# Column product of the Fourier layers: seven block products for two row tiles instead of eight

## The chip, the cores and the metric

The kernel runs on one core of one Trainium2 chip. The time is the device time of one launch in microseconds, the median of several runs. TensorE (PE) multiplies, VectorE (DVE), ScalarE (ACT) and GpSimd (POOL) do the elementwise work, and SyncE's queue (SP) starts all transfers.

## The reference

Four layers on x (2048 rows, 640 columns): attention, Fourier, attention, Fourier. What matters here is the Fourier layer:

```python
def _B_ref(x, dft_seq_re, dft_seq_im, dft_hid_re, dft_hid_im):
    a = jnp.einsum("bsd,ed->bse", x, dft_hid_re)
    b = jnp.einsum("bsd,ed->bse", x, dft_hid_im)
    y = jnp.einsum("ts,bse->bte", dft_seq_re, a) - jnp.einsum("ts,bse->bte", dft_seq_im, b)
    return y
...
x = x + _A_ref(_layernorm(x, axis=-1), A_wqkv, A_wo)
x = x + _B_ref(_layernorm(x, axis=-1), B_dft_seq_re, B_dft_seq_im, B_dft_hid_re, B_dft_hid_im)
```

All is in float32. The kernel multiplies with the two sequence matrices first and with the two hidden matrices second.

## The kernel before, in words

Every float32 product is made of three products of rounded parts: each operand is cut into a high part (ACT copies it to a rounding type) and a low part (DVE or POOL subtracts the high part), and high times high, high times low and low times high are added in PSUM (`split`, `product3`).

In a Fourier layer the sequence product comes first (`seq`, `gather`). It leaves u in DRAM (`ud`), with two parts, real and imaginary, each 640 by 2048, columns of u standing for rows of the result. Then comes the column product, `fourier` from line 1401: for each of 16 row tiles of 128 rows, `hidden(t)` multiplies ten 128-blocks of u (five of each part) with ten rows of weights `wc` of 640 columns. It does so in two halves of 320 columns, 30 matmuls each (ten blocks, three products), each half into its own PSUM bank of the role "y" (banks 5, 6, 7, 0 in turn). DVE adds the old row of x (L1414), and SP stores the row (L1415).

A group g is two row tiles, 256 columns of u. `load_u(g, part)` (L1335) brings 640 KB of u into one of three places in `kp[1]`; `cut_u` cuts it with one wide ACT copy (L1348) and a DVE subtraction (L1351), a group ahead of its use.

What sets the order: the program is written out in the order in which the loops emit it, each engine and the SP queue takes its own instructions in that order, and semaphores make an instruction wait for what it reads or overwrites. The tile buffers are reused in turn. In the first Fourier layer (`more`) the loop also begins the next attention layer: `prep_load`, `prep_stats`, `prep_norm` from t = 8 on, and transposes (`prep_turn`) from t = 12 on. In the last layer there is nothing beside the column product.

At the end of the sequence product, `gather` adds the last accumulators (L1270: DVE and POOL), and SP stores u from them (L1267) before it starts the next loads of u.

Of the kernel before, what the change touches and what calls it, by code (L numbers as in the profile page):

```python
# [15 lines left out]
P = 128  # L16
S = 2048
D = 640
KC = D // P
# [4 lines left out]
NB = S // P  # L24
# [30 lines left out]

def pairs(c):
    return [(c[2 * i], c[2 * i + 1]) for i in range(len(c) // 2)]


class Net:  # L60
# [66 lines left out]
    def next(self, name):  # L127
        i = self.turn.get(name, 0)
        self.turn[name] = i + 1
        tiles = getattr(self, name)[:3]  # L130
        return tiles[i % len(tiles)]
# [1203 lines left out]
            self.nc.sync.dma_start(p, self.ud[part, :, :, g * 256:(g + 1) * 256].rearrange("k p t -> p k t"))  # L1335
            self.u_raw[g, part] = p

    def cut_u(self, g, part):
        if g < NB // 2:
            src = self.u_raw.pop((g, part))  # L1340
            his, los = self.ubuf[g % 2][part]
            for out, sub_of in ((his, None), (los, his)):
                k = 0
                for t in out:
                    n = t.shape[1] // 256
                    t = t.rearrange("p (k t) -> p k t", t=256)
                    if sub_of is None:
                        self.nc.scalar.activation(t, src[:, k:k + n], AF.Copy)  # L1348
                    else:
                        h = his[0][:, k * 256:(k + n) * 256].rearrange("p (k t) -> p k t", t=256)  # L1350
                        self.nc.vector.tensor_tensor(out=t, in0=src[:, k:k + n], in1=h.bitcast(F32), op=OP.subtract)  # L1351
                    k += n
            self.u[g % 2][part] = [sum([cuts(t, 256) for t in out], []) for out in (his, los)]

    def fourier(self, xsrc, xdst, more):
        nc = self.nc
        wc = pairs(sum([cuts(t, D) for t in self.big[:2]], []) + cuts(self.qp[0][:, :4 * D], D))
        self.u_raw, self.u = {}, [{}, {}]
        loads = []

        def weights(ks):
            for k in ks:
                r, d = divmod(k, KC)
                loads.append(self.load_w({k: wc[k]}, self.a[("wr", "wi")[r]], [d], neg=r == 1, at=k))

        def step_w():

            if len(loads) > 1 or (loads and self.begun):
                if not self.begun:
                    next(loads[0])  # L1370
                    self.begun = True
                else:
                    if len(loads) > 1:
                        next(loads[1])
                    next(loads.pop(0))
                    self.begun = bool(loads)

        self.begun = False
        total = len(self.order)
        for n in range(self.un, total):  # L1380
            if n == total - NB:
                weights(range(8))
            if n == total - NB // 2:
                weights(range(8, 10))
                self.take_qk("kp", 1, F32)
            self.seq(n)
            step_w()
            if n >= total - 5 and n < total - 2:
                self.load_u((n - total + 5) // 2, (n - total + 5) % 2)
            if n == total - 2:  # L1390
                self.pt = [self.slot_tile(f"pt{i}", 1536, F32R) for i in range(4)]
                qc = cuts(self.qp[1], 1280)
                self.ubuf = [[[[self.pt[2 * r + l][:, :1280]] for l in range(2)] for r in range(2)],
                             [[[qc[0]], [qc[1]]], [[qc[2]], [self.vq[0], self.vq[1], self.rr[0][:, :256]]]]]
                self.cut_u(0, 0)
                self.cut_u(0, 1)
        self.leave()
        while loads:
            step_w()

        self.hid = True

        def hidden(t):
            x = self.raw()
            nc.sync.dma_start(x, xsrc[t * P:(t + 1) * P, :])
            xw = self.raw()
            rs = slice(t % 2 * P, (t % 2 + 1) * P)
            us = self.u[t // 2 % 2]
            for hf in range(2):
                p = self.bank("y", 320)  # L1410
                cs = slice(hf * 320, (hf + 1) * 320)
                self.all3(p, [((us[k // KC][0][k % KC][:, rs], us[k // KC][1][k % KC][:, rs]),
                               (wc[k][0][:, cs], wc[k][1][:, cs])) for k in range(2 * KC)])
                nc.vector.tensor_tensor(out=xw[:, cs], in0=p, in1=x[:, cs], op=OP.add)  # L1414
            nc.sync.dma_start(xdst[t * P:(t + 1) * P, :], xw)  # L1415

        for t in range(NB):
            if more and t == 8:
                self.tmp = cuts(self.kp[0], D)
                self.home = [self.home[i] for i in (2, 3, 0, 1)]  # L1420
            if more and 8 <= t < 11:
# [5 lines left out]
            if more and 11 <= t < NB - 1:  # L1427
# [4 lines left out]
            if more and t == NB - 1:  # L1432
                self.prep_stats(8)
                self.prep_norm(8)
            g = t // 2 + 1
            if t % 2 == 0:
                if g == 1:
                    self.cut_u(g, 0)
                    self.load_u(g, 1)
                    self.load_u(g + 1, 0)  # L1440
                    hidden(t)
                    self.cut_u(g, 1)
                else:
                    hidden(t)
                    self.cut_u(g, 0)
                    self.load_u(g + 1, 0)
            else:
                if g > 1:
                    self.cut_u(g, 1)
                self.load_u(g + 1, 1)  # L1450
                hidden(t)
            if more and t >= 12:
                if i < 2:
                    self.cut_chunk(i)
                for k in range(2):
                    self.prep_turn(2 * i + k)
                if i < 3:
                    for k in range(2):
                        self.prep_load(xdst, 6 + 2 * i + k)
        self.ready, self.hid = 8, False  # L1460


# [70 lines left out]
```

## Time and profile before

| | |
|---|---|
| median of 3 runs | 2297.08 us (2295.49 to 2301.15) |
| profiled execution | 2298.78 us, its span 2297.1 us |
| busy in the span: PE, DVE, ACT, POOL | 95%, 65%, 46%, 44% |
| column product of the first Fourier layer | from about 1012.7 to 1153.5 us, PE busy 139.15 of 140.80 us |
| column product of the last layer | from about 2153 to 2294 us, PE busy 140.38 of 141.00 us |
| mean granted TensorE clock | 0.99 of full |

In the profile, PEld is the loading of weights into PE's array, which runs beside the matmuls. A row of the timeline gives start, duration, engine, line, operation, what is written from what, shape and count, and in brackets how long the engine had been idle before and what ended that.

### The profile page before, as it was taken

Reading aid. Unit: us, or ns where it says so; the run is one execution under the profiler, and the core shown is the slowest. Engines: PE = TensorE matmul, PEld = TensorE weight load, DVE = VectorE, ACT = ScalarE, POOL = GpSimd, SP = SyncE. Lnnn points to the kernel's source line nnn. Section 1 sums busy time; section 2 is a strip of 40 time slices with the busy share of each in tenths; the row PEclk is TensorE's granted clock in tenths of the full one; section 3 lists DMA queues with packets and bytes.
Section 4 is the critical chain, followed back from the end, with each engine's and each line's share of the span. In section 5 each row is a group of like instructions: output and inputs, shape, how many; then the busy total and the mean of one; then the engine's idle time right before and its main releaser. Section 6 shows DMA issues by size and latency. Waiting matters only on the chain.

```text
span 2297.1 us, 49411 instructions
## 1 busy us (share of the span) xinstructions
PE 2188.9 (95%) x18064; PEld 1809.5 (79%) x18064; DVE 1498.1 (65%) x3705; ACT 1066.1 (46%) x1825; POOL 1006.3 (44%) x1540
## 2 busy tenths in 40 slices
PE   7999999899889999999999999999989899999999
PEld 7976666677758888889999766666777688888899
DVE  6347777775687868772451677777756968688622
ACT  2116666655554545541331366666555545445310
POOL 3036666767743223230130566668677332331300
PEclk9999999999999999999999999999999999999999
DMA  5545555774435353655445455657744344546542
GB/s 189 174 149 174 179 165 189 220 219 159 137 120 172 124 186 129 220 167 171 151 167 180 160 176 166 188 181 222 212 151 136 114 166 137 179 143 213 165 165 98
DMA packets 217299, 385.59 MB, mean 168 GB/s; under 512 B 38880, under 2 KB 85472, under 8 KB 217056
## 3 DMA queue, kind: packets, MB, share of 16 engines
q1 hardware_dynamic: 217056, 382.43, 51.6%
q8 instruction: 143, 2.34, 0.4%
q14 instruction: 100, 0.82, 0.1%
HBM read 267.39 MB, written 113.77 MB: 166 GB/s over the span
## 4 chain that ended last, share of the span: by engine, by line
PE 36%; POOL 6%; ACT 3%; issue 2%; DVE 2%; DMA 1%; SPq 0%; ACTq 0%; POOLq 0%; DVEq 0%
PE banks L1226 14%; PE banks L169 12%; PE banks L187 4%; PE banks L570 2%; ACT pt L579 2%; PE banks L604 2%; PE banks L541 1%; POOL pt L585 1%; POOL big L162 1%; POOL pt L589 1%; POOL c L473 1%; DMA qp<-qk_d 1%; POOL x L775 0%; POOL kp L162 0%; PE banks L269 0%
## 5 line engine op out<-in xcount | busy, mean ns | idle before, releaser
L546 DVE CUSTOM_DVE_ANT_0 ux<-banks,mask 128x384 bf16<-128x384 f32 (+2 forms) x1024 | 545.5, 533 | 218.7 <-PE banks L541 99.4
L579 ACT ACTIVATE pt<-banks 128x768 f32<-128x768 f32 (+2 forms) x512 | 394.7, 771 | 299.5 <-PE banks L570 150.6
L585 POOL TENSOR_SCALAR_AFFINE_SELECT pt<-pt 128x256 f32<-128x256 f32 x512 | 208.3, 408 | 236.0 <-ACT pt L579 230.8
L187 PE MATMUL banks<-big,wc 64*128 64x512 f32 x1920 | 278.7, 396 | 0.4 <-DVE pt L370 0.4
L570 PE MATMUL banks<-qp,kp 61*128 61x384 f32 (+2 forms) x1024 | 229.7, 408 | 38.5 <-ACT pt L579 32.1
L570 PEld LDWEIGHTS banks<-qp,kp 61*128 61x128 f32 x1024 | 110.4, 184 | 153.2 <-ACT pt L579 145.0
L604 PE MATMUL banks<-pt,vq 128*32 128x128 f32 x5760 | 216.2, 277 | 7.9 <-POOL pt L585 7.8
L187 PEld LDWEIGHTS banks<-big,wc 64*128 64x128 f32 x1920 | 199.9, 186 | 15.7 <-DVE pt L370 0.5
L541 PE MATMUL banks<-kp,qp 60*128 60x384 f32 (+2 forms) x1024 | 207.7, 341 | 3.3 <-DVE mc L546 3.2
L604 PEld LDWEIGHTS banks<-pt,vq 128*32 128x32 f32 x5760 | 143.5, 109 | 64.1 <-issue 30.9
L162 DVE TENSOR_TENSOR qp<-pt,qp 128x512 fp32r<-128x512 f32 (+1 forms) x199 | 154.7, 792 | 59.7 <-ACT qp L156 58.0
L589 POOL TENSOR_SCALAR_AFFINE_SELECT pt<-pt 128x256 f32<-128x256 f32 x448 | 183.3, 409 | 0.0
L156 ACT ACTIVATE qp<-pt 128x512 fp32r<-128x512 f32 (+1 forms) x201 | 124.1, 625 | 120.8 <-DVE pt L1156 32.6
L1226 PE MATMUL banks<-qp,big 128*128 128x512 f32 x648 | 155.5, 394 | 3.1 <-POOL big L162 3.1
L1155 POOL TENSOR_TENSOR pt<-pt,pt 128x512 f32<-128x512 f32 x40 | 59.4, 1490 | 216.4 <-DMA pt<-c 162.2
L1414 DVE TENSOR_TENSOR x<-banks,x 128x320 f32<-128x320 f32 x64 | 29.7, 488 | 181.7 <-DMA x<-x_d 105.4
L156 ACT ACTIVATE c<-pt 128x512 fp32r<-128x512 f32 x144 | 89.2, 625 | 121.5 <-POOL pt L1144 56.5
L1226 PEld LDWEIGHTS banks<-qp,big 128*128 128x128 f32 x648 | 121.6, 190 | 29.2 <-POOL big L162 4.5
L541 PEld LDWEIGHTS banks<-kp,qp 60*128 60x128 f32 x1024 | 130.6, 186 | 12.5 <-DVE mc L546 7.3
L162 DVE TENSOR_TENSOR c<-pt,c 128x512 fp32r<-128x512 f32 x142 | 111.6, 791 | 33.0 <-ACT c L156 30.2
L169 PE MATMUL banks<-big,pt 128*128 128x320 f32 x768 | 119.3, 311 | 1.6 <-DVE pt L1351 1.0
L1226 PE MATMUL banks<-qp,xc 128*128 128x512 f32 x480 | 117.0, 393 | 0.0
(202 smaller groups left out, 4412.6 us busy)
## 6 DMA issues: line engine op xcount, KB each, us to landing
pt<-c SPq DMA_DIRECT2D x188, 512.0 KB
qk_d<-c SPq DMA_DIRECT2D x80, 512.0 KB
kp<-qk_d SPq DMA_DIRECT2D x384, 80.0 KB
qp<-qk_d SPq DMA_DIRECT2D x384, 80.0 KB
kp<-u_d SPq DMA_DIRECT2D x32, 640.0 KB
o_d<-ou SPq DMA_DIRECT2D x64, 256.0 KB
x_d<-x SPq DMA_DIRECT2D x48, 320.0 KB
v_d<-pt SPq DMA_DIRECT2D x16, 768.0 KB
```

What stands on the lines that cost most here:

```text
L156: nc.scalar.activation(hi, src, AF.Copy, scale=-1.0 if neg else 1.0)
L162: (eng or nc.vector).tensor_tensor(out=lo, in0=src, in1=hi.bitcast(F32), op=OP.subtract)
L169: self.nc.tensor.matmul(p, x, y, start=n == 0, stop=n == last)
L187: self.nc.tensor.matmul(ps[a], x[r], y[r], start=half + i == 0, stop=half == 1 and i == n - 1, skip_group_check=True)
L541: nc.tensor.matmul(p, qp[quad % 2][b:b + 60, z, qb * P:(qb + 1) * P], kp[quad % 2][b:b + 60, z, k0 * P:(qb + 1) * P], start=True, stop=True)
L546: nc.vector.tensor_tensor_reduce(out=self.ux[:, :n * P], in0=p, in1=self.mask[:, 384 - n * P:], scale=1.0, scalar=NEG, op0=OP.add, op1=OP.max,
L570: nc.tensor.matmul(p, kp[quad % 2][b:b + 61, z, kb * P:(kb + 1) * P], qp[quad % 2][b:b + 61, z, kb * P:(kb + n) * P], start=True, stop=True)
L579: nc.scalar.activation(pt[quad, kb][:, 2 * z:2 * z + 2, :n * P], self.banks[:, 0:2, :n * P], AF.Exp, scale=SCALE)
L585: nc.gpsimd.affine_select(out=t[:, :, 0:P], in_=t[:, :, 0:P], pattern=[[0, 2], [1, P]], compare_op=OP.is_ge, fill=0.0, base=0, channel_mul ...
L589: nc.gpsimd.affine_select(out=t[:, :, 256:384], in_=t[:, :, 256:384], pattern=[[0, 2], [-1, P]], compare_op=OP.is_gt, fill=0.0, base=0, ch ...
L604: nc.tensor.matmul(acc[quad, bk][32 * h:32 * h + 32, at:at + P], vq[:, 96 * (kb % 4) + 21 * h:96 * (kb % 4) + 21 * h + 32], t[:, h, (qb - ...
L1226: nc.tensor.matmul(self.banks[:, bk, :], p, b[q], start=start and m == 0, stop=stop and last and m == 2, skip_group_check=True)
```

## The change

Two row tiles of u and the weight rows are taken as two-by-two blocks: A (rows z = 0, 1; parts real, imaginary) times B (part; column half of 320). Eight block products become seven, with sums of blocks of A (s1, s4 and two made in place), sums of blocks of B (`w_sum`: t1 to t4), and sums of the products. A block product is 15 matmuls (five blocks, three products). `sevens` names the groups that are done so: 1 to 5 in the first Fourier layer, 1 to 7 in the last. The others (group 0, and 6 and 7 of the first layer) go by `eight`.

Operands are now made one block at a time by `operands`, a generator; `make(4)` keeps four made operands ahead of the product that PE is given. The weights are loaded once more, raw, after the weights `wc` are ready (`load_sums`), and `make_sums` forms and cuts the sums during group 0. x is added in place, and rows are loaded some ahead (`load_x`). The diff, cut:

```diff
-    def cut_u(self, g, part):
...
+    def cut_part(self, src):
+
+        his, los = self.upl[self.n_upl % len(self.upl)]
+        self.n_upl += 1
+        for t, k, n in self.tiles_of(his):
+            self.nc.scalar.activation(t, src(k, n), AF.Copy)
+        for (t, k, n), (h, _, _) in zip(self.tiles_of(los), self.tiles_of(his)):
+            self.nc.vector.tensor_tensor(out=t, in0=src(k, n), in1=h.bitcast(F32), op=OP.subtract)
+        return [sum([cuts(t, P) for t in ps], []) for ps in (his, los)]
...
+    def operands(self, g, wino):
...
+        a11, a21, a12, a22 = q(0, 0), q(0, 1), q(1, 0), q(1, 1)
+        if not wino:
+            for a in (a11, a12, a21, a22):
+                yield self.cut_part(a)
+            return
+        yield self.cut_part(a11)
+        s1, s4 = of(self.u_s1), of(self.u_s4)
+        both(a21, a22, self.u_s1, OP.add, nc.gpsimd)
+        nc.vector.tensor_tensor(out=a21(0, KC), in0=a21(0, KC), in1=a11(0, KC), op=OP.subtract)
+        for t, k, n in self.tiles_of(self.u_s1):
+            nc.vector.tensor_tensor(out=a11(k, n), in0=a11(k, n), in1=t, op=OP.subtract)
+        both(a12, a11, self.u_s4, OP.add, nc.gpsimd)
+        pieces = [(t, k, n) for t, k, n in self.tiles_of(self.u_s4)]
+        yield self.cut_sum(s4, pieces)
+        yield self.cut_part(a12)
+        yield self.cut_part(a11)
+        yield self.cut_part(a21)
+        yield self.cut_sum(s1, pieces)
+        yield self.cut_part(a22)
...
+    def make_sums(self, k):
...
+        r, i = self.w_raw[k]
+        (r1, r2), (i1, i2) = cuts(r, 320), cuts(i, 320)
+        nc.gpsimd.tensor_tensor(out=r1, in0=r2, in1=r1, op=OP.subtract)
+        nc.gpsimd.tensor_tensor(out=r2, in0=r2, in1=i2, op=OP.add)
+        nc.vector.tensor_tensor(out=i2, in0=i2, in1=r1, op=OP.add)
+        nc.vector.tensor_tensor(out=i1, in0=i2, in1=i1, op=OP.subtract)
+        hi, lo = self.w_sum[k]
+        for n, t in enumerate((r, i)):
+            self.parts_of(hi[:, n * D:(n + 1) * D], lo[:, n * D:(n + 1) * D], t)
...
+        sevens = range(1, 6 if more else NB // 2)
+        steps = ((g, n, g in sevens) for g in range(NB // 2) for n in range(7 if g in sevens else 4))
...
+        def eight(t, sums):
+            ops = [made.popleft() for _ in range(2)]
+            make(ahead)
             for hf in range(2):
                 p = self.bank("y", 320)
                 cs = slice(hf * 320, (hf + 1) * 320)
...
+                for k in sums[hf]:
+                    self.make_sums(k)
+                add(nc.vector, raws[t][:, cs], p, raws[t][:, cs])
+            store_x(t)
+
+        def seven(g, halfway):
+            y, z, v, x = [self.banks[:, b, :320] for b in ROLES["y"]]
+            (x11, x12), (x21, x22) = [cuts(raws[t], 320) for t in (2 * g, 2 * g + 1)]
+            p1, u2, u3 = self.u_sum
...
+            def product(p, name, start=True):
+                hi, lo = made.popleft()
+                make(ahead)
...
+            product(x, "b11")
+            self.load_u(g + 1, 1)
+            nc.scalar.activation(p1, x, AF.Copy)
+            product(v, "b22")
+            add(nc.vector, x22, x22, v, OP.subtract)
+            product(x, "b21", start=False)
+            add(nc.vector, x11, x, x11)
+            halfway()
+            product(y, "t2")
+            add(nc.vector, u2, y, p1)
+            add(nc.gpsimd, x12, u2, x12)
+            product(z, "t3")
+            add(nc.vector, u3, z, u2)
+            add(nc.gpsimd, x21, u2, x21)
+            add(nc.gpsimd, x22, u3, x22)
+            product(v, "t1", start=False)
+            add(nc.vector, x12, v, x12)
+            store_x(2 * g)
+            add(nc.vector, x22, v, x22)
+            product(z, "t4", start=False)
+            add(nc.vector, x21, z, x21)
+            store_x(2 * g + 1)
...
+        self.load_u(1, 1)
+        load_x(0, 1)
+        sums = self.load_sums()
+        next(sums)
+        self.load_u(2, 0)
+        for _ in sums:
+            pass
...
+                    eight(2 * g + z, ((), ()) if g else (((), (0,)), ((1, 2), (3, 4)))[z])
```

`self.u_s1` and `self.u_s4` each lie in two pieces, 512 and 128 columns, so an instruction over them is two. `cut_sum` is `cut_part` in these two pieces. In `product` the 15 matmuls stand behind `make(ahead)`.

More of the change, by code (lines that the diff above doesn't have):

```diff
@@ L1336, in load_u, with quarter @@
             self.u_raw[g, part] = p
-    def cut_u(self, g, part):
[L1339 to L1353, printed above, removed]
+    def quarter(self, g, part, z):
+        return self.u_raw[g, part][:, :, z * P:(z + 1) * P]
@@ new lines, in tiles_of @@
+    @staticmethod
+    def tiles_of(ps):
+        k = 0
+        for t in ps:
+            n = t.shape[1] // P
+            yield t.rearrange("p (k t) -> p k t", t=P), k, n
+            k += n
+    def cut_part(self, src):
[6 more added lines that the diff above has]
+        return [sum([cuts(t, P) for t in ps], []) for ps in (his, los)]
@@ new lines, in add_parts, with q, of, both @@
+    def add_parts(self, eng, out, a, b, op):
+        for t, k, n in self.tiles_of(out):
+            eng.tensor_tensor(out=t, in0=a(k, n), in1=b(k, n), op=op)
+    def operands(self, g, wino):
+        def q(part, z):
+            a = self.quarter(g, part, z)
+            return lambda k, n: a[:, k:k + n]
+        def of(ps):
+            ts = list(self.tiles_of(ps))
+            return lambda k, n: next(t[:, k - k0:k - k0 + n] for t, k0, n0 in ts if k0 <= k and k + n <= k0 + n0)
+        def both(a, b, ps, op, eng):
+            for t, k, n in self.tiles_of(ps):
+                eng.tensor_tensor(out=t, in0=a(k, n), in1=b(k, n), op=op)
+        nc = self.nc
+        a11, a21, a12, a22 = q(0, 0), q(0, 1), q(1, 0), q(1, 1)
[17 more added lines that the diff above has]
+        yield self.cut_part(a22)
@@ new lines, in cut_sum @@
+    def cut_sum(self, src, pieces):
+        his, los = self.upl[self.n_upl % len(self.upl)]
+        if len(his) > 1:
+            return self.cut_part(src)
+        self.n_upl += 1
+        hi, lo = [t[0].rearrange("p (k t) -> p k t", t=P) for t in (his, los)]
+        for _, k, n in pieces:
+            self.nc.scalar.activation(hi[:, k:k + n], src(k, n), AF.Copy)
+        for _, k, n in pieces:
+            self.nc.vector.tensor_tensor(out=lo[:, k:k + n], in0=src(k, n), in1=hi[:, k:k + n].bitcast(F32), op=OP.subtract)
+        return [sum([cuts(t, P) for t in ps], []) for ps in (his, los)]
@@ new lines, in load_sums @@
+    def load_sums(self):
+        c = [self.work.tile([P, 2, 512], F32, name="wt", tag="c", bufs=3).rearrange("p l c -> p (l c)")[:, :D]
+             for _ in range(3)]
+        w = cuts(self.take_qk("kp", 0, F32), 2 * D)
+        self.w_raw = [c[:2]] + [cuts(t, D) for t in w[:3]] + [[c[2], self.raw()]]
+        for k, ts in enumerate(self.w_raw):
+            for n, t in zip(("wr", "wi"), ts):
+                self.nc.sync.dma_start(t, self.a[n][:, k, :])
+            yield
+    def make_sums(self, k):
+        nc = self.nc
+        if k == 0:
+            self.w_sum = sum([pairs(cuts(self.take_big(2 + i), 2 * D)) for i in range(2)], [])
+            self.w_sum.append([self.work.tile([P, 2, D], F32R, name="wt", tag="wc").rearrange("p l c -> p (l c)")
+                               for _ in range(2)])
+        r, i = self.w_raw[k]
[7 more added lines that the diff above has]
+            self.parts_of(hi[:, n * D:(n + 1) * D], lo[:, n * D:(n + 1) * D], t)
@@ L1357, in fourier, with make @@
         wc = pairs(sum([cuts(t, D) for t in self.big[:2]], []) + cuts(self.qp[0][:, :4 * D], D))
-        self.u_raw, self.u = {}, [{}, {}]
+        self.u_raw, self.n_upl = {}, 0
+        sevens = range(1, 6 if more else NB // 2)
+        steps = ((g, n, g in sevens) for g in range(NB // 2) for n in range(7 if g in sevens else 4))
+        made, making = deque(), [None]
+        def make(n):
+            while len(made) < n:
+                g, i, wino = next(steps, (None,) * 3)
+                if g is None:
+                    return
+                if i == 0:
+                    making[0] = self.operands(g, wino)
+                made.append(next(making[0]))
         loads = []
@@ L1401, in fourier, with load_x, store_x, add @@
         self.hid = True
[L1403 to L1408, printed above, removed]
+        raws = {}
+        def load_x(*ts):
+            for t in ts:
+                if t < NB and t not in raws:
+                    raws[t] = self.raw()
+                    nc.sync.dma_start(raws[t], xsrc[t * P:(t + 1) * P, :])
+        def store_x(t):
+            nc.sync.dma_start(xdst[t * P:(t + 1) * P, :], raws.pop(t))
+        def add(eng, out, a, b, op=OP.add):
+            eng.tensor_tensor(out=out, in0=a, in1=b, op=op)
+        ahead = 4
+        def eight(t, sums):
+            ops = [made.popleft() for _ in range(2)]
+            make(ahead)
             for hf in range(2):
@@ L1411, in hidden @@
                 cs = slice(hf * 320, (hf + 1) * 320)
-                self.all3(p, [((us[k // KC][0][k % KC][:, rs], us[k // KC][1][k % KC][:, rs]),
+                self.all3(p, [((ops[k // KC][0][k % KC], ops[k // KC][1][k % KC]),
                                (wc[k][0][:, cs], wc[k][1][:, cs])) for k in range(2 * KC)])
[L1414 to L1418, printed above, removed]
+                for k in sums[hf]:
+                    self.make_sums(k)
@@ L1419, in fourier, with before @@
+        def before(t):
+            if not more:
+                return
+            if t == 8:
                 self.tmp = cuts(self.kp[0], D)
                 self.home = [self.home[i] for i in (2, 3, 0, 1)]
-            if more and 8 <= t < 11:
+            if 8 <= t < 11:
                 for k in range(2):
@@ L1426, in fourier @@
             i = t - 12
-            if more and 11 <= t < NB - 1:
+            if 11 <= t < NB - 1:
                 for k in range(2):
@@ L1431, in fourier, with behind @@
                     self.prep_norm(2 * i + 2 + k)
-            if more and t == NB - 1:
+            if t == NB - 1:
                 self.prep_stats(8)
                 self.prep_norm(8)
[L1435 to L1451, printed above, removed]
+        def behind(t):
             if more and t >= 12:
+                i = t - 12
                 if i < 2:
@@ L1459, in fourier @@
                         self.prep_load(xdst, 6 + 2 * i + k)
+        self.load_u(1, 1)
[5 more added lines that the diff above has]
+            pass
+        self.u_sum = [self.slot_tile(n, 512, F32)[:, :320] for n in ("rr1", "rr2", "vq2")]
+        for g in range(NB // 2):
+            if g and g not in sevens:
+                self.load_u(g + 1, 1)
+            load_x(2 * g + 1, 2 * g + 2)
+            if not more or g < 4:
+                load_x(2 * g + 3)
+            before(2 * g)
+            if g in sevens:
+                seven(g, lambda: before(2 * g + 1))
+            else:
+                for z in range(2):
+                    if z:
+                        before(2 * g + 1)
+                    eight(2 * g + z, ((), ()) if g else (((), (0,)), ((1, 2), (3, 4)))[z])
+                    behind(2 * g + z)
+            if g:
+                self.load_u(g + 2, 0)
         self.ready, self.hid = 8, False
```

23 lines of the change are left out of this document (18 added, 5 removed).

## The prediction, made before the result was known

> **What bounds the kernel now.** I read the page first (engines, chain), then the table of stretches over both column products, then the timeline inside them, and last the groups by shape for the price of each kind of instruction. The page names the bound, TensorE:
>
> ```profile
> span 2297.1 us, 49411 instructions
> PE 2188.9 (95%) x18064; PEld 1809.5 (79%) x18064; DVE 1498.1 (65%) x3705; ACT 1066.1 (46%) x1825; POOL 1006.3 (44%) x1540
> ```
>
> The stretches (us, then busy time of PE, PEld, DVE, ACT and POOL, granted clock, DMA share, GB/s) show the two column products:
>
> ```profile
> 1012.70:1153.50 140.80, 139.15 (x943) 138.57 (x942) 51.60 (x96) 31.63 (x38) 16.74 (x22) 0.99 0.50 168
> 1030.30:1048.00 17.70, 17.70 (x123) 17.70 (x122) 4.75 (x7) 2.55 (x2) 0.00 (x0) 1.00 0.67 212
> 2153.00:2294.00 141.00, 140.38 (x958) 140.12 (x956) 38.23 (x58) 16.57 (x13) 5.67 (x3) 1.00 0.44 145
> ```
>
> PE never rests there; DVE, ACT and POOL are mostly idle. So fewer matmuls would pay in full, but only if the other engines, which get the new work, never make PE wait. The price of a matmul, from two bursts of the timeline:
>
> ```profile
> 1012.92 3.68 PE L169 MATMUL banks<-big,pt 128*128 128x320 f32 x24
> ...
> 1017.31 3.68 PE L169 MATMUL banks<-big,pt 128*128 128x320 f32 x24
> ```
>
> One half of a row tile is 30 matmuls; the bursts begin 4.39 us apart, so a matmul takes 0.147 us, a block product of 15 takes 2.2 us and two row tiles (120 matmuls) 17.6 us.
>
> **Removed: matmuls.** Seven products of 15 instead of eight: 105 matmuls, 15.4 us, 2.2 us less per group. `sevens` holds groups 1 to 5 of the first Fourier layer and 1 to 7 of the last, 12 groups: -26.4 us. That is the whole gain.
>
> **Added: elementwise work.** Prices (mean ns of one in the groups by shape, the second column in the timeline):
>
> ```profile
> 1001.57 0.81 DVE L162 TENSOR_TENSOR xc<-big,xc 128x640 fp32r<-128x640 f32 x1
> 1002.31 0.42 DVE L162 TENSOR_TENSOR vq<-big,vq 128x256 fp32r<-128x256 f32 x1
> 1003.25 0.68 DVE L162 TENSOR_TENSOR c<-pt,c 128x512 fp32r<-128x512 f32 x1
> 1003.44 0.63 ACT L156 ACTIVATE c<-pt 128x512 fp32r<-128x512 f32 x1 [0.87 <-PE banks L1226]
> ...
> L162 DVE TENSOR_TENSOR big<-banks,big 128x128 fp32r<-128x128 f32 x32 | 9.0, 280 | 0.0
> L156 ACT ACTIVATE big<-banks 128x128 fp32r<-128x128 f32 x32 | 8.8, 276 | 0.4 <-PE banks L269 0.4
> L1414 DVE TENSOR_TENSOR x<-banks,x 128x320 f32<-128x320 f32 x64 | 29.7, 488 | 181.7 <-DMA x<-x_d 105.4 <-PE banks L169 76.2
> L1155 POOL TENSOR_TENSOR vq<-pt,vq 128x512 f32<-128x512 f32 x8 | 10.3, 1293 | 40.0 <-DMA pt<-c 27.2 <-DVE kp L1289 5.4 <-ACT xc L156 4.9
> L1018 POOL TENSOR_TENSOR s<-big 128x256 f32<-128x256 f32 x16 | 11.9, 747 | 0.0
> ```
>
> DVE: 640 columns 0.81, 512 0.68, 128 0.28, and 320 out of SBUF 0.48 (between the 256 and 512 rows); 320 out of PSUM 0.49. POOL: 512 columns 1.29, 320 0.89 and 128 0.48, both on the line through its 512 and 256 rows. Per seven-product group DVE has seven cuts, three subtracting instructions of the chain below and seven additions, about 11 us of 15.4; ACT and POOL less. By totals it fits. Two places break by order.
>
> **The chain in front of the fifth product.** Each engine takes its instructions in the order written. `product` pops one operand and makes the one four ahead, so the fifth product (t3) makes the second operand of the next group. Its turn emits everything between the two first `yield`s of `operands`: POOL a21+a22, DVE a21-a11 in place (it overwrites what POOL reads), DVE a11-s1, POOL a12+a11, then ACT's and DVE's cut of s4. Only behind it stands DVE's `u3 = z + u2`, and the seventh product (t4) adds into bank z, so it may not begin before u3 has read it. On POOL the chain stands behind `x12 + u2`, which needs the fourth product. So the chain cannot begin early. Counted from the moment PE is free of the fourth product; the first step, from the last rows of the timeline: the add starts 0.35 us behind its last matmul's start, 0.2 behind PE being free.
>
> ```profile
> 2293.07 0.31 PE L169 MATMUL banks<-qp,rr 128*128 128x320 f32 x1
> 2293.42 0.49 DVE L1414 TENSOR_TENSOR x<-banks,x 128x320 f32<-128x320 f32 x1 [2.90 <-PE banks L169]
> ```
>
> u2 ends at 0.2+0.49 = 0.7; POOL x12 1.6; POOL a21+a22 (1.29+0.48) 3.4; DVE a21 4.2; DVE a11 in two pieces 4.9 and 5.2; POOL a12+a11, first piece from 4.9 to 6.2, with 0.3 lost beside DVE's second piece 6.5, second piece 7.0; DVE's cut, 0.68+0.28, would start at 7.1 but shares with POOL's `x21 + u2` (7.0 to 7.9) and ends about 8.9; u3 9.4. PE has only products five and six to fill that, 4.4 us. It waits 5.0 us in every group that prepares another seven-group: groups 1 to 4 of the first layer, 1 to 6 of the last, ten times: **+50 us**. Such a group takes 20.4 us instead of 17.6. The sharing rests on this pair, POOL and DVE side by side with both inputs in SBUF:
>
> ```profile
> 1011.85 7.31 POOL L1270 TENSOR_TENSOR kp<-kp 128x512 f32<-128x512 f32 x4 [14.83 <-DVE kp L1270]
> 1012.37 3.04 DVE L1270 TENSOR_TENSOR kp<-kp 128x512 f32<-128x512 f32 x2
> ```
>
> DVE took 1.52 us each where 0.68 is its price, POOL 1.83 against 1.29: nearly one after the other. Ends: 3.9 us per group without sharing; 7.0 with POOL at 1.83 throughout and a load late by a microsecond. What hides an addition that is not in this list (x22, x11, the ACT copy p1) is a product of 2.2 us each.
>
> **The weight sums in group 0.** Group 0's last half uses bank 0, and the first product of group 1 writes bank 0 again (role "y": 5, 6, 7, 0). So it needs the last addition of group 0, and `eight` puts that addition behind all five `make_sums` on DVE. Ahead of these stands the first chain, which needs u of group 1, second part. That load's place:
>
> ```profile
> 1019.55 1.07 SPq L1335 DMA_DIRECT2D kp<-u_d  x2
> 1025.41 1.27 ACT L1348 ACTIVATE qp<-kp 128x1280 fp32r<-128x1280 f32 x1 [13.25 <-DMA kp<-u_d]
> 2151.36 7.31 POOL L1270 TENSOR_TENSOR kp<-kp 128x512 f32<-128x512 f32 x4 [14.87 <-DVE kp L1270]
> 2163.80 1.27 ACT L1348 ACTIVATE qp<-kp 128x1280 fp32r<-128x1280 f32 x1 [12.13 <-DMA kp<-u_d]
> ```
>
> PE began the stage at 1012.92, so it lands at 12.5 us of the stage (11.4 in the last layer, where the same POOL instruction starts at 2151.36, and 1011.85 here was 1.07 us ahead of the stage). From 12.5: POOL 1.8, DVE 0.8+0.7+0.3, POOL's second sum overlapping DVE's last piece, 17.5; ACT and DVE cut 18.6. Then DVE in order: four additions (2.0), two cuts (1.6), five times two 320-column sums and two 640-column cuts (2.58 each, 12.9): 35.1. POOL's ten sums of 0.89 use the same memory path: 44 if all add up. I take 42, nearer that end, since the L1270 pair shows almost full serialization and only the four additions from PSUM leave room. PE is ready at 17.6: it waits 24.4 us, and 23.3 in the last layer: **+48 us** (ends 34 and 52). The 14 loads added or moved here, about 5 MB through SP, would take 24 us at the 212 GB/s quoted above, done near 31 of the stage: ahead of the last sum's turn, so at nothing; late, they would add to the 42.
>
> **The granted clock.** Where PE rested in this stage, its clock fell:
>
> ```profile
> 1121.55 0.56 PE L169 MATMUL banks<-big,pt 128*128 128x320 f32 x2 [0.68 <-ACT pt L1348]
> 1123.08 1.29 PE L169 MATMUL banks<-big,pt 128*128 128x320 f32 x7 [0.97 <-DVE pt L1351]
> 1124.21 1.75 PE L169 MATMUL banks<-qp,pt 128*128 128x320 f32 x6
> 1125.76 4.55 PE L169 MATMUL banks<-big,pt 128*128 128x320 f32 x24
> ...
> 1130.14 1.04 PE L169 MATMUL banks<-qp,pt 128*128 128x320 f32 x6
> ...
> 1125.00:1126.00 1.00, 1.00 (x5) 1.00 (x5) 0.97 (x4) 0.00 (x0) 0.57 (x1) 0.50 1.02 312
> ```
>
> After two rests of under a microsecond the clock was 0.50, and the next bursts took 1.75 for 1.04 and 4.55 for 3.68: 1.6 us lost. Twelve longer waits at 1.5 us: **+18 us**; ends 0 (the clock is back before the wait ends) and 2.2 each, 26. The Trainium skill (TensorE: Matmul & The Clock Gate, Part 1) says that the clock halves after at least one idle window of about 3.4 us. By that rule an estimate is that about half of the 5 us waits hold a whole window, and this term would be 10 instead of 18. The row speaks for the larger: it fell here without such a window.
>
> **Sum.** -26.4 + 50 + 48 + 18 = +89.6 us. The rows come from the profiled execution, which took 2298.8 us (its span of 2297.1 and 1.7 around it) and so lies 1.7 above the median of the runs, 2297.1: 2298.8 + 89.6 - 1.7 = 2386.7, rounded to 2387 us. By the low ends -26.4+39+34+0 = +47, 2344; by the high ends -26.4+70+52+26 = +122, 2419. An end of the kernel that moves costs nothing: the last add and its store stand behind the last matmul as before.
>
> **Rivals.** *Faster: the elementwise work keeps ahead.* If an engine started whatever is ready, u3 and group 0's additions would not wait behind the preparation, and all 26.4 us would be kept: 2271 us. It decides at total waits of 26.4 us. For it: DVE's 38 us busy of 141 in the last layer's stage. Against it: both waits are dependencies plus written order, and 9.4 against 4.4 leaves a wide gap. *Only group 0 waits*: the chains end inside 4.4 us; -26.4+48+3 of clock, 2320. It needs each chain at under half my sum. *Only the chains wait*: the weight sums finish by 17.6 us; -26.4+50+15, 2336. Against it: DVE's own 16.5 us behind a load at 12.5. *Transfers take over*: u of the next group, second part, waits on SP behind x loads whose buffers wait for stores, and lands after POOL is free, 2 us more in ten chains: 2407. The load took 5.9 us above, and it has about 8.
>
> **How the numbers follow.** Forecast 0.69, faster 0.06, only group 0 0.06, only chains 0.08, transfers 0.11. Range 2336 to 2420: from the only-chains rival to the high ends, leaving out the faster rival and only group 0, and what of the transfers lies beyond. A measurement can tell 0.3%, 7 us, from no change; only a near balance of waits and gain lands inside: 0.01. Faster by more 0.06, slower by more 0.93.
>
> **What would show it.** PE with 12 times 15 matmuls fewer; in the middle groups an idle PE of about 5 us ahead of the seventh product, put down to DVE's u3, with POOL's and DVE's chain steps alternating before it; about 24 us of idle PE at the start of group 1 behind DVE's last addition of group 0; granted clock near 0.5 after both. Wrong if PE runs from product to product, if u3 stands ahead of the chain, or if group 1 starts near 18 us of the stage.

## The result and the profile after

The changed kernel is slower: 2390.32 us median (2384.37 to 2398.99, 4 runs) against 2297.9 (2295.49 to 2301.15, 4 runs), a ratio of 1.0404 with a 95% interval of 1.0364 to 1.0444. The profiled execution took 2384.37 us, its span 2382.7. The page of the changed kernel begins so:

```profile
span 2382.7 us, 49678 instructions
PE 2184.8 (92%) x17884; PEld 1805.1 (76%) x17884; DVE 1609.3 (68%) x3900; ACT 1116.0 (47%) x1956; POOL 1104.4 (46%) x1644
```

PE has 18064 - 17884 = 180 matmuls fewer, 12 times 15, as forecast. But its share fell from 95% to 92%. The stretches over both column products (us, then busy time of PE, PEld, DVE, ACT, POOL, granted clock, DMA share, GB/s) show where:

```profile
1010.50:1175.00 164.50, 119.49 (x729) 118.07 (x728) 88.23 (x154) 45.03 (x82) 54.30 (x58) 0.85 0.44 153
1010.50:1049.45 38.95, 17.77 (x122) 17.52 (x120) 27.77 (x37) 9.74 (x16) 20.38 (x18) 0.79 0.55 201
2191.50:2379.00 187.50, 141.16 (x856) 139.24 (x854) 97.97 (x164) 43.07 (x82) 61.49 (x63) 0.86 0.37 126
```

The stretches are not cut at the same events as those of before, and both stretches of the first layer end ahead of its last matmul, so their lengths are not subtracted. Counted from the first to the last matmul, the column product of the first layer takes 191.3 us instead of 147.8, that of the last layer 187.3 instead of 140.8. PE, which had rested 1.65 us in the first and not at all in the last, now rests 45 us in the first and 46 in the last, and the granted clock is 0.85 and 0.86. The list of waits of the changed kernel (us in total, times, longest) names what PE waited for:

```profile
PE banks L1549 <- DVE vq L1514: 49.4, 11, 5.9
PE banks L1549 <- DVE x L1514: 41.8, 2, 21.2
```

`vq` is the tile of u3: eleven waits ahead of the seventh product. The second row is the two long ones at the start of group 1. One group of the changed kernel in the timeline, from the fourth product's addition u2 on, shows the first kind:

```profile
1060.31 0.49 DVE L1514 TENSOR_TENSOR rr<-banks,rr 128x320 f32<-128x320 f32 x1 [0.98 <-PE banks L1549]
1060.93 0.88 POOL L1514 TENSOR_TENSOR x<-rr,x 128x320 f32<-128x320 f32 x1 [22.08 <-issue]
1061.78 1.30 POOL L1376 TENSOR_TENSOR ou<-kp 128x512 f32<-128x512 f32 x1
...
1063.52 0.82 DVE L1387 TENSOR_TENSOR kp<-kp 128x640 f32<-128x640 f32 x1 [2.72 <-POOL kp L1376]
1064.07 0.60 PE L1549 MATMUL banks<-wt,pt 128*128 128x320 f32 x3
1064.38 0.69 DVE L1389 TENSOR_TENSOR kp<-kp,ou 128x512 f32<-128x512 f32 x1
...
1065.15 1.26 POOL L1376 TENSOR_TENSOR ou<-kp 128x512 f32<-128x512 f32 x1 [1.66 <-DVE kp L1389]
...
1067.11 1.08 DVE L1408 TENSOR_TENSOR pt<-ou,pt 128x512 fp32r<-128x512 f32 x1 [1.84 <-ACT pt L1406]
...
1068.32 0.48 DVE L1514 TENSOR_TENSOR vq<-banks,rr 128x320 f32<-128x320 f32 x1
...
1068.94 3.54 PE L1549 MATMUL banks<-big,pt 128*128 128x320 f32 x12 [4.27 <-DVE vq L1514]
```

POOL and DVE hand the chain to each other, u3 (the row at 1068.32) stands last, PE has run out at 1064.5. Then 12 matmuls take 3.54 us where they take 1.92 at full clock. The second kind, the last rows of group 0:

```profile
1048.08 0.83 DVE L162 TENSOR_TENSOR wt<-x,wt 128x640 fp32r<-128x640 f32 x1
...
1048.82 0.48 DVE L1514 TENSOR_TENSOR x<-banks,x 128x320 f32<-128x320 f32 x1
...
1049.45 5.54 PE L1549 MATMUL banks<-big,qp 128*128 128x320 f32 x24 [21.18 <-DVE x L1514]
```

The fifth weight sum is cut, only then comes group 0's last addition, and PE starts at once behind it.

### The profile page after: what moved, and what is told of

The parts are those of the page before. It is cut to its first block, busy times and chain, and to the rows that moved or that the text cites. A ratio compares the mean times of both kernels' runs of the same rounds, so it can differ in the third digit from the quotient of the medians.

```text
span 2382.7 us, 49678 instructions
## 1 busy us (share of the span) xinstructions
PE 2184.8 (92%) x17884; PEld 1805.1 (76%) x17884; DVE 1609.3 (68%) x3900; ACT 1116.0 (47%) x1956; POOL 1104.4 (46%) x1644
## 3 DMA queue, kind: packets, MB, share of 16 engines
q8 instruction: 141, 2.31, 0.4%
## 4 chain that ended last, share of the span: by engine, by line
PE 30%; POOL 7%; issue 6%; ACT 3%; DVE 3%; DMA 1%; SPq 1%; ACTq 0%; POOLq 0%; DVEq 0%
PE banks L1226 12%; PE banks L169 6%; PE banks L187 4%; PE banks L570 2%; ACT pt L579 2%; PE banks L1549 2%; PE banks L604 2%; PE banks L541 1%; POOL pt L585 1%; POOL big L162 1%; POOL pt L589 1%; POOL ou L1376 0%; POOL c L473 0%; POOL x L1514 0%; POOL kp L162 0%
## 5 line engine op out<-in xcount | busy, mean ns | idle before, releaser
L1549 PE MATMUL banks<-big,qp 128*128 128x320 f32 x462 | 85.7, 343 | 60.7 <-DVE x L1514 41.8
L1549 PEld LDWEIGHTS banks<-big,qp 128*128 128x128 f32 x462 | 80.6, 218 | 62.1 <-ACT rr L1355 52.9
```

The costliest lines, as they stand in the source:

```text
L1549: nc.tensor.matmul(p, a[k], b, start=start and k + n == 0, stop=k == KC - 1 and n == 2, skip_group_check=True)
```

## The experiments

All times stand beside runs of the kernel before on the same chip, whose medians were 2297 to 2302 us.

**The three terms, each by itself.** *The rest of the change.*

```diff
-        sevens = range(1, 6 if more else NB // 2)
+        sevens = range(0)
```

The raw weights are not loaded and no sums are made either.

> No group goes by seven products, no weight sums and no raw weights are loaded; all else of the change stays (operands cut block by block, x in place, order of loads). Theory: the loss lies in the chain and in the sums alone, so this runs like the kernel before, 2293 to 2305 us. Rival 'the smaller cuts and the new order of loads cost by themselves': 2315 or more.

Measured: 2295.19 us, a ratio of 0.9981 (0.9969 to 0.9993). The new operand scheme costs nothing; if anything it gains 0.2%. In its trace the two rests of PE that the kernel before had in the first column product (0.68 and 0.97 us) are gone, and that product takes 144.1 us instead of 147.8.

*The granted clock.* Idle matmuls in PE's waits:

```diff
+        def keep(n):
+            for i in range(n):
+                nc.tensor.matmul(self.banks[:, 2, :320], wc[0][0][:, :P], wc[0][0][:, :320], start=i == 0, stop=i == n - 1,
...
+            if g + 1 in sevens:
+                keep(28)
             product(z, "t4", start=False)
...
+                if g == 0:
+                    keep(140)
```

> The kernel after, with matmuls that nobody reads put into PE's waits: 28 (4.1 us) ahead of the seventh product in the ten groups with a chain, 140 (20.5 us) ahead of group 1, into a bank that is free there. They neither start nor end a wait. Theory 'granted clock': the clock stays at 1.0, and the 18 to 20 us that the products after the waits lose in the kernel after come back: 2368 to 2376 us. Rival 'the products behind a wait are slow for another reason (first use of operands, bank turnaround)': no change, 2385 to 2395, or a few us more where the added matmuls run past a wait.

Measured: 2372.59 us, ratio 1.0327 (1.0308 to 1.0345), 17.7 us under the changed kernel by the medians, its mean granted clock 0.989 against 0.972. In its timeline the seventh product still starts when u3 lets it, but runs at full clock:

```profile
2244.84 4.27 PE L1579 MATMUL banks<-big 128*128 128x320 f32 x28
2249.35 1.99 PE L1549 MATMUL banks<-big,pt 128*128 128x320 f32 x12 [0.24 <-DVE vq L1514]
```

Adding 560 matmuls made the kernel faster: the clock term is shown, and shown apart from the waits. Inside the two column products the profiled executions differ by 21.1 us (357.5 and 378.6); the rest of the kernel, where nothing was changed, was 9.3 us longer in this execution.

*POOL beside DVE in group 0.* POOL's two sums per weight row are left out, so t1 to t4 are other numbers; nothing else changes.

```diff
-        nc.gpsimd.tensor_tensor(out=r1, in0=r2, in1=r1, op=OP.subtract)
-        nc.gpsimd.tensor_tensor(out=r2, in0=r2, in1=i2, op=OP.add)
```

> POOL's two sums per weight row in group 0 are left out (the sums are then other numbers), DVE's and ACT's work stays. Theory 'DVE and POOL take turns at SBUF': DVE is through about 5 us earlier, the wait ahead of group 1 falls from 21 to 16 us in both layers, about 2380 us. Rival 'DVE's own work and its turns with ACT set the wait': 2388 to 2392, the wait at 20 us or more.

Measured: 2376.17 us, ratio 1.0338 (1.0321 to 1.0354). In the timeline of PE the waits ahead of group 1 are 15.13 and 16.38 us instead of 21.18 and 20.66: POOL's sums cost 6.1 and 4.3 us of wait, half to two thirds of their 8.9 us. The changed kernel's timeline shows where: two of DVE's cuts of the first sum while POOL works, and two behind POOL's last sum. In the kernel without POOL's sums the cuts of the first sum take 1.71 us as well, with ACT's copies beside them as before; so it is POOL, and not the turns with ACT, that makes DVE slower.

```profile
1031.40 2.88 DVE L162 TENSOR_TENSOR big<-wt,big 128x640 fp32r<-128x640 f32 x2
...
1041.68 1.71 DVE L162 TENSOR_TENSOR big<-kp,big 128x640 fp32r<-128x640 f32 x2
```

*Order of the addition in group 0.*

```diff
+                add(nc.vector, raws[t][:, cs], p, raws[t][:, cs])
                 for k in sums[hf]:
                     self.make_sums(k)
-                add(nc.vector, raws[t][:, cs], p, raws[t][:, cs])
```

> In group 0 DVE's addition of a half stands ahead of the weight sums emitted with that half instead of behind them. Theory 'order on DVE': group 1's first product begins when the third sum is cut, about 6 us earlier, and the wait for the rest moves to the fourth product, the first to read the sums; 6 to 8 us less in each Fourier layer, about 2377 us. Rival 'the transfers of the raw weights are late': the same idle time in all, 2385 to 2395.

Measured: 2381.25 us, ratio 1.0348 (1.0322 to 1.0373), and in its list of waits:

```profile
PE banks L1549 <- DVE x L1514: 30.4, 2, 15.3
```

5.7 us less at each of the two places on average, and no new wait at the fourth product, where the theory had put one: the place of the addition was part of the price, the sums' work most of it.

**Where the chain's wait goes when it is taken away.** *u3 no longer gates the seventh product:*

```diff
-            add(nc.gpsimd, x21, u2, x21)
+            add(nc.gpsimd, x21, u3, x21)
...
-            product(z, "t4", start=False)
-            add(nc.vector, x21, z, x21)
+            product(y, "t4")
+            add(nc.vector, x21, y, x21)
```

> The last product of a group (t4) goes into bank y with its own start instead of being added into bank z, so it no longer has to wait for u3; x21 takes u3 and y instead of u2 and z. Theory 'chain in front of u3': the 4.4 us wait before the seventh product is gone in ten groups; in its place the second product of the next group waits about 1.9 us for the last addition from bank v, which still stands behind the chain on DVE. So 25 us less by the waits and up to 20 more if the clock no longer falls: 2345 to 2365 us. Rival 'DVE, ACT and POOL cannot keep up by their totals': the wait moves to another product at full size, 2385 to 2395.

Measured: 2380.58 us, ratio 1.0347 (1.0315 to 1.038). *POOL's first sum one product earlier:*

```diff
-        yield self.cut_part(a11)
         s1, s4 = of(self.u_s1), of(self.u_s4)
         both(a21, a22, self.u_s1, OP.add, nc.gpsimd)
+        yield self.cut_part(a11)
```

> POOL's first sum of the chain (a21+a22) is emitted with the first operand of the next group, one product earlier and ahead of POOL's x12 addition. Theory 'chain': the chain is shorter by POOL's x12 and this sum, 2.7 us, so the wait before the seventh product falls from 4.4 to about 1.8 us in ten groups: 2345 to 2364 us. Rival 'the load of u is the last to arrive': the sum waits for its load where it stands, DVE and POOL are no earlier, 2385 to 2395. Rival 'totals': no change.

Measured: 2386.68 us, ratio 1.0376 (1.0347 to 1.0405). *Both together:*

> Both edits. Theory 'chain': no wait is left in the ten groups (the chain ends 5.5 us after the fourth product, the next use is 8.8 us after it), 44 us of waits and their share of clock, 15 to 20 us, come back: 2325 to 2335 us; what is left over the kernel before is the two long waits at the start of group 1 less 26 us of matmuls. Rival 'totals': 2370 or more.

Measured: 2377.7 us, ratio 1.0331 (1.0306 to 1.0356). All three gained far less than I expected. With the first edit the wait did move to the second product of the next group, but it is 2.31 to 4.85 us there, not 1.9. Part of it is that DVE's addition of v to x22 waits 1.2 us there for POOL's addition of u3 to the same row, which POOL takes up only behind x21. With the second, the first chain of the last layer behaves as forecast (2.05 us) and the later ones do not, in PE's timeline:

```profile
2248.41 3.11 PE L1549 MATMUL banks<-big,pt 128*128 128x320 f32 x12 [2.05 <-DVE vq L1514]
2270.56 3.54 PE L1549 MATMUL banks<-big,vq 128*128 128x320 f32 x12 [4.98 <-DVE vq L1514]
```

The timeline of the kernel with both edits shows why, a load and the sum that needs it:

```profile
2256.07 0.37 SPq L1335 DMA_DIRECT2D kp<-u_d  x1
...
2263.31 1.29 POOL L1376 TENSOR_TENSOR ou<-kp 128x512 f32<-128x512 f32 x1 [11.01 <-DMA kp<-u_d]
```

POOL was ready, u was not: SP had issued the load late, behind the stores of the group before and loads of x, and it took 7.2 us. In the changed kernel this sum has no such wait in eight of the ten chains, since the chain's own wait gives the load time; in the other two it waits 0.2 and 1.6 us. So the rival of the transfers was there, for the most part hidden behind the chain. The next edit puts it to the test, on top of both. It also lets DVE add v to x22 ahead of POOL's addition, so it tests the two together:

```diff
             product(x, "b11")
             self.load_u(g + 1, 1)
+            ahead_x(g)
...
             product(x, "b21", start=False)
+            self.load_u(g + 2, 0)
...
-            add(nc.gpsimd, x22, u3, x22)
...
             add(nc.vector, x22, v, x22)
+            add(nc.gpsimd, x22, u3, x22)
...
-            load_x(2 * g + 1, 2 * g + 2)
...
-            if g:
+            if g and g not in sevens:
                 self.load_u(g + 2, 0)
```

> On top of both chain edits: SP gets the loads of u one product after their place is free, ahead of the loads of x and of the stores; DVE adds v to x22 before POOL adds u3. Theory: behind the chain the next two waits are the late load of u (POOL's first sum waited for it 7 us after its issue) and bank v; with both gone the ten waits are gone, 2325 to 2335 us. Rival 'totals of DVE, ACT and POOL': still a wait of 3 us or more in each group, 2360 or more.

Measured: 2335.17 us, ratio 1.0169 (1.0148 to 1.019). The ten waits are down to 1.5 us or less, but for one of 3.97; group 5's is 3.15; and 42 of the 44 us in this row of its list of waits are the two long ones:

```profile
PE banks L1549 <- DVE x L1514: 44.0, 5, 21.3
```

So DVE, ACT and POOL have room for seven products in about 15.4 us by their totals; order and the load's time were the bound. Which share of the gain is the load's and which the addition's was not tried.

**Toward a better version.** *The sums over two groups:*

```diff
-        sevens = range(1, 6 if more else NB // 2)
+        sevens = range(2, 6 if more else NB // 2)
...
-                    eight(2 * g + z, ((), ()) if g else (((), (0,)), ((1, 2), (3, 4)))[z])
+                    eight(2 * g + z, ((), ()) if g > 1 else ((((), (0,)), ((), (1,))), (((2,), ()), ((3,), (4,))))[g][z])
```

> The kernel after with seven products from group 2 on instead of 1 and the five weight sums spread over groups 0 and 1. Theory 'the sums wait because group 0 is too short for them': both long waits ahead of the first seven-group (42 us) and their clock loss (about 4 us) go, at the price of one group less by seven products in each layer and one chain wait less: 2390 - 46 + 4 - 12 = about 2336 to 2350. Rival 'the sums' work itself disturbs the stage wherever it stands': 2365 or more.

Measured: 2369.33 us, ratio 1.0298 (1.0276 to 1.0321): missed. Two waits of 15.1 us stay ahead of the first seven-group. In its timeline DVE is done with sum 1 and its cuts at 1035.8 and then stands still, since the chain is next in its order and its load has just been issued:

```profile
1035.38 0.39 SPq L1335 DMA_DIRECT2D kp<-u_d  x1
...
1040.37 1.29 POOL L1376 TENSOR_TENSOR ou<-kp 128x512 f32<-128x512 f32 x1 [9.46 <-DMA kp<-u_d]
...
1042.11 0.82 DVE L1387 TENSOR_TENSOR kp<-kp 128x640 f32<-128x640 f32 x1 [6.37 <-POOL kp L1376]
```

The remaining three sums come behind it. By this timeline what was missing was, again, an earlier load; no run moves that load alone. *All edits so far, and group 5's row statistics behind its last addition* (this diff and the next two show only what is new in them):

```diff
             add(nc.vector, x11, x, x11)
-            halfway()
...
             add(nc.vector, x21, y, x21)
+            halfway()
             store_x(2 * g + 1)
```

> Chain edits, loads of u ahead on SP, sums over two groups behind the additions, and the next layer's row statistics of group 5 moved behind the group's last addition. Theory: ten groups by seven products keep 2.2 us each, 22 us, and the late loads of u still cost about 1 us in some groups: 2278 to 2292 us, faster than the kernel before. Rival 'totals': 2300 or more.

Measured: 2313.64 us, ratio 1.006 (1.0041 to 1.0079): missed, with waits of 10.8 us at the first seven-group of each layer and one of 4.59 in group 4. *Another order of the products* (b11, b22, t2, t3, b21, t1, t4) with the additions ahead of the sums; u3 is then emitted ahead of the chain:

```diff
-        yield self.cut_part(a12)
         yield self.cut_part(a11)
         yield self.cut_part(a21)
+        yield self.cut_part(a12)
...
+            product(z, "t3")
+            add(nc.vector, u3, z, u2)
...
+            product(x, "b21", start=False)
+            add(nc.vector, x11, x, x11)
...
+            if g in sevens:
+                self.load_u(g + 1, 1)
```

> As the one with all edits, but the products of a group go in the order b11, b22, t2, t3, b21, t1, t4: u3 then stands ahead of the chain on DVE, and the place of u is free two products earlier, so that its load starts at the group's start. Theory: no wait left in the groups, 2298 - 22 = 2276, within 2272 to 2284 us. Rival: DVE and POOL in turns are too slow for 15.4 us a group, 2290 or more.

Measured: 2319.68 us, ratio 1.0085 (1.006 to 1.011): missed, with the same long waits (10.9 and 11.5 us), and 1.2 us or a little more in every group. Most of these small ones end with a cut on ACT (L1355); they were not followed further. *Seven products from group 3 on, the load for the first chain a group earlier:*

```diff
+        sevens = range(3, 6 if more else NB // 2)
...
             make(ahead)
+            if t < 6 and t % 2 < 2 and t not in (0, 5):
+                self.load_u(t // 2 + 2, t % 2)
...
             ahead_x(g)
+            before(2 * g)
             nc.scalar.activation(p1, x, AF.Copy)
...
+                    eight(2 * g + z, (((), (0,)), ((), (1,)), ((), (2,)), ((3,), (4,)))[2 * g + z] if 2 * g + z < 4 else ((), ()))
```

> On the kernel with all edits (2314 us): seven products only from group 3 on, the weight sums spread over groups 0 and 1, the loads of u for the first seven-group issued a group earlier, and in each seven-group the next layer's loads put behind the load of u. Theory: the 10.8 us waits ahead of the first seven-group (a chain behind a late load, then sums) and the 4.6 us wait of group 4 are gone; eight groups keep 2.2 us each: 2298 - 17.6 and some 5 us of small waits, 2280 to 2292 us, below the kernel before. Rival 'DVE and POOL in turns have no room for the sums in any place': a wait of 8 us or more remains at group 3, 2300 or more.

Measured: **2283.79 us** against 2297.4, ratio 0.9947 (0.9932 to 0.9961): faster than both. The rows of its PE timeline in which PE waited 0.2 us or more inside the two column products are these:

```profile
1069.19 2.43 PE L1551 MATMUL banks<-big,pt 128*128 128x320 f32 x15 [0.68 <-DVE x L1514]
1118.36 3.76 PE L169 MATMUL banks<-big,qp 128*128 128x320 f32 x24 [2.40 <-DVE x L1514]
...
2199.94 2.43 PE L1551 MATMUL banks<-big,pt 128*128 128x320 f32 x15 [0.68 <-DVE x L1514]
2250.47 2.53 PE L1551 MATMUL banks<-big,qp 128*128 128x320 f32 x9 [1.90 <-DVE x L1514]
```

Eight groups at 2.2 us are 17.6 us; it is 13.6 us faster than the kernel before. Not all of that comes from the seven products: the kernel with only the new operand scheme had a ratio of 0.9981, so about 8 us are theirs. The traces say the same: the two column products take 288.6 us in the kernel before, 284.9 with only the new scheme, 275.7 here. This last edit moves several things at once, and which of them ended the long waits was not separated.

## Why the prediction was right

The forecast was 2387 us, the median is 2390.3. The profiled executions differ by 2384.4 - 2298.8 = 85.6 us: the two column products by 90.0 (43.5 and 46.5, first to last matmul), the rest of the kernel by -4.4. That rest is the same work in all runs, and in the fourteen profiled executions it took 2003.7 to 2013.4 us, so the -4.4 is not put down to the change. The prediction's sum, +89.6, is about the column products. There the terms measure:

- Matmuls: -26.4 us, 180 fewer, as put.
- Chain: ten waits of 44.5 us in sum (4.26 to 5.86 each). The list counts them from the modelled end of the last matmul, 0.16 us behind PE being free (three matmuls show 0.60 us: two steps of 0.147 and 0.31), so 46 us. Forecast 50. The chain took 8.8 us from PE being free (1060.1 to 1068.9) where I summed 9.4: POOL's second sum ended 0.3 us earlier than summed, and DVE's cut of s4 lost 0.3 us less beside POOL.
- Sums: 41.8 us in two waits, 42 with the same 0.16. Forecast 48. Group 1 began 38.9 us into the stage instead of 42. Two parts of it: the load landed at 11.4 instead of 12.5, and POOL's sums cost a little over half of their own time, not nearly all. My reading of the pair L1270 as full serialization was too strong: POOL ran ahead and was through at 1038.9, and from there DVE worked at its own prices.
- Clock: 26.7 us. By so much the matmuls behind the thirteen waits, from start to start, exceed 0.147 us each. Forecast 18, twelve times 1.5. This term was mis-sized most, and lies just past its high end of 26: a wait cost 2.1 us on average, where the two short rests that I took it from had cost 1.6 together. Behind one wait:

```profile
1068.94 3.54 PE L1549 MATMUL banks<-big,pt 128*128 128x320 f32 x12 [4.27 <-DVE vq L1514]
1072.28 1.00 PE L1549 MATMUL banks<-wt,pt 128*128 128x320 f32 x3
1073.08 4.05 PE L1549 MATMUL banks<-big,pt 128*128 128x320 f32 x24
1076.97 1.04 PE L1549 MATMUL banks<-qp,pt 128*128 128x320 f32 x6
```

  From start to start 12, 3 and 24 matmuls take 3.34, 0.80 and 3.89 us; their price is 1.76, 0.44 and 3.52. The kernel with matmuls in its waits got 21.1 us of its column products back; the difference of the medians, 17.7, holds the scatter of the rest as well.
- Missed: a wait of 4.9 us, 5.1 with the same 0.16, in group 5 of the first layer, which I put at nothing, since its next group has no chain. It prepares rows of the next attention layer there, and ACT's four normalizations stand ahead of the cut that DVE needs before u2, in the changed kernel's timeline:

```profile
1153.28 0.83 ACT L229 ACTIVATE kp<-kp,nm 128x640 f32<-128x640 f32 x1 [7.60 <-POOL nm L228]
...
1157.22 0.82 DVE L1357 TENSOR_TENSOR pt<-kp,pt 128x640 fp32r<-128x640 f32 x1 [4.81 <-ACT pt L1355]
```

- Missed too: a gain of 3.7 us. The prediction says that PE never rests in the column products, but rows that it quotes show two rests in the first one and slow matmuls behind them. They go with the new operand scheme, as the kernel with only that scheme shows.

The sum is -26.4 + 46.1 + 42.2 + 26.7 + 5.1 - 3.7 = 90.0, as measured. The two kinds of wait and what ends them were right, as forecast. Their sizes were less good: two terms were 4 and 6 us too high, one was 9 too low, and +5 and -4 were forgotten. That these cancel to 0.4 us is luck.

The rivals: neither "only group 0 waits" nor "only the chains wait" was so, both are in the list. "The engines keep ahead" fell with the rows above. "Transfers take over" happened in one of the ten chains, that of group 4, where POOL waited for u and PE's wait is 5.86 us instead of about 4.3:

```profile
1129.50 1.29 POOL L1376 TENSOR_TENSOR ou<-kp 128x512 f32<-128x512 f32 x1 [1.56 <-DMA kp<-u_d]
```

It happened more often as soon as the chain was shortened.

The rule of the Trainium skill (TensorE: Matmul & The Clock Gate, Part 1), by which the clock halves after at least one idle window of about 3.4 us, would by the prediction's estimate have put the clock's loss at 10 us. The trace does not agree: the loss is 26.7 us, the matmuls were slow behind all thirteen waits and not behind half of the short ones, and in the wait shown in the last section the clock fell about 2.6 us after PE ran out.

The observation to look for, u3 last behind alternating POOL and DVE steps, was there step by step.

## What to carry to other kernels

When work is moved from the bounding engine to idle ones, their totals say little: write down, for each point where the bounding engine must wait, which instructions stand ahead of the releasing one on its own engine, and sum that chain against the time that the bounding engine can fill. A wait that is removed uncovers the next one, here a load that the wait itself had hidden, so an edit is judged with the queue of loads moved along with it. And a rest of PE costs more than its length, as the clock comes back late.

## What the runs showed of the hardware that was not expected

Filling a wait with matmuls that nobody reads makes the kernel faster. In the changed kernel, PE ran out at 1064.5 us, the clock fell shortly after 1067, and PE, which started again at 1068.94, ran 5 us at half clock. In one-microsecond stretches (the granted clock stands ahead of the DMA share):

```profile
1066.00:1067.00 1.00, 0.00 (x0) 0.00 (x0) 0.00 (x0) 0.56 (x2) 1.00 (x3) 1.00 0.00 0
1067.00:1068.00 1.00, 0.00 (x0) 0.00 (x0) 0.89 (x1) 1.00 (x4) 0.64 (x1) 0.54 0.00 0
...
1069.00:1070.00 1.00, 1.00 (x4) 1.00 (x5) 0.93 (x2) 0.16 (x1) 1.00 (x1) 0.50 0.00 0
...
1073.00:1074.00 1.00, 1.00 (x6) 1.00 (x5) 0.68 (x2) 0.00 (x0) 0.00 (x0) 0.55 0.00 0
1074.00:1075.00 1.00, 1.00 (x9) 1.00 (x8) 0.54 (x1) 0.00 (x0) 0.00 (x0) 1.00 0.35 120
```

Waits of nearly the same length, 4.26 to 4.28 us, cost between 1.4 and 2.7 us of clock; what decides between these was not tried. The changed kernel's four runs lie between 2384 and 2399 us, and the longest had the lowest mean clock, 0.964 against 0.972 of the profiled one. The kernel before spread over 12 us itself in one round of eleven runs (2293.4 to 2305.5), so it is not shown that the change widens the spread. The load of 640 KB of u took 5.0 us from its issue to the first use in one of the rows above and 7.2 in another, where SP had issued another load of u and two of x in the two microseconds before it.
